# Loading wv by chunks of the model dimension, and V of the first tiles chunk by chunk, in a fused attention and SwiGLU kernel

## The chip, the cores and the metric

The kernel runs on one core of a Trainium2 chip. A core has five instruction streams that run side by side: TensorE (PE in the profile, with its weight loads as PEld), VectorE (DVE), ScalarE (ACT), GpSimd (POOL) and SyncE (SP), which here only issues DMAs. The metric is the device time of one execution in microseconds, as the median of the runs shown. The profile is of one execution.

## What is computed

The input x (2048 tokens, model dimension D = 640, bfloat16) is normalized once, and the result feeds a linear attention of 32 heads of 20 and a SwiGLU layer of 1536, which are added to x.

```python
xn = layernorm(x)                                   # over the 640 columns
q, k, v = split(xn @ wqkv)                          # wqkv: 640 x 1920; v is its last 640 columns
pq, pk  = q @ w_phi, k @ w_phi                      # per head, 20 x 20
phi_q   = concat(softmax(pq), softmax(-pq))         # 40 features to a head
phi_k   = concat(softmax(pk), softmax(-pk))
kv, z   = phi_k.T @ v, sum(phi_k)
A       = ((phi_q @ kv) / (phi_q @ z + 1e-6)) @ wo
B       = (silu(xn @ w1) * (xn @ w3)) @ w2
out     = x + A + B
```

## The kernel before

**Tiles.** The 2048 tokens are 16 tiles of 128. `x_tok` holds a tile with its tokens on the partitions; normalized there, it is transposed to `xnT`, where the model dimension lies on the partitions in DC = 5 chunks of 128. Every projection of a tile is a sum over these five chunks, accumulated in PSUM: `xnT[:, i, tile]` is the stationary operand, rows `i` of the weight are the moving one. PSUM has eight banks of 512 float32 columns, and 640 columns take two of them.

**The order of the work.** No loop order is written out. 14 generators (`norms`, `transposes`, `attention`, `mlps` and so on, from line 729) each offer their next step, a list of instructions; the loop from line 927 works out when each could start, by the planner's own costs (line 353 for a matmul: columns / 2400 + 0.003; 0.06 for a transpose, line 357) and 0.07 for an engine to learn that another is done, and takes the earliest, the stream with the lower rank in a tie. A step with PE work counts as startable at the latest of its operands and PE's free time plus 0.15 (line 945). The steps of `norms` are taken well ahead (`URGENT`, line 921). A step is never split. The instructions of each engine are then played in that order, with semaphore waits where they depend on another engine or a DMA; an engine also waits for its own earlier instruction if it reads what that one writes (line 146).

**The start.** `first_loads` (line 412) issues on SP, in this order: half of x tile 0, tiles 1 and 2, the first part of wv, tile 3, the second part of wv, the first third of w1 and w3, w_phi, the transposing load of wk, and x tiles 4 to 11; the other half of tile 0 goes out on ACT. `warm_up` gives PE filling matmuls on zeros while it waits. `norms` (line 729) works out mean and variance of tiles 0, 2 and 3 on DVE with two `bn_stats` of half a tile each (`ln_half`, line 449) and a `bn_aggr` (in `ln_rstd`, line 453), of tile 1 on ACT; the power -0.5 is POOL's. `ln_apply` (line 492) normalizes the tile in place on DVE. `xn_transpose` (line 511) transposes tiles 0 to 3 on PE and copies the result from PSUM on the engine that the planner expects to be done first; later tiles are transposed by DMA. After tile 0's transposes PE gets eight more filling matmuls.

**V of tiles 0 to 3.** In `attention` (line 814) tiles 0 to 3 are handled apart from the rest: for each tile, once it is transposed, two banks are held, and ten steps `v_part` (line 552) of one matmul each follow, first the five chunks of columns 0 to 383, then the five of columns 384 to 639. This goes with the load: wv comes by columns, all five chunks of columns 0 to 383 first. The 640 results lie one behind the other, from column 128 of the first bank on, so that 384 of them end with it. `v_store` (line 556) copies them to `v2` on ACT. Later tiles use `v_tile` (line 560): ten matmuls of 320 columns, one half of the columns to a bank, and a store over both banks.

After V of tile 3 come two columns of the MLP, the folding of w_phi into wk, and the K projections.

Of the kernel before, what the change touches and what calls it, by code (L numbers as in the profile page):

```python
# [3 lines left out]
ACT = mybir.ActivationFunctionType  # L4
# [5 lines left out]
D = 640  # L10
H = 32
DH = 20
F = 1536
T = S // 128
DC = D // 128
# [232 lines left out]
def bass_parallel_sum__linear_kernel_hedgehog__glu_gated_swiglu__prompt_kernel(  # L248
# [16 lines left out]
    P = _Program(nc)  # L265
# [12 lines left out]
    def new(name, shape, dtype, offset=None):  # L278
        size = mybir.dt.size(dtype)
        for n in shape[1:]:  # L280
            size *= n
        return P.sbuf(name, shape, dtype, region(size) if offset is None else offset)
# [13 lines left out]
    xnT = new("xnT", [128, DC, S], bf)  # L296
# [14 lines left out]
    wv = new("wv", [128, DC, D], bf, RKV + 6400)  # L311
# [14 lines left out]
    v2 = new("v2", [128, T, H * 21], bf, RV)  # L326
# [15 lines left out]
    def bank(k, cols=512, off=0, rows=128):  # L342
        return PS[0:rows, k * 512 + off:k * 512 + off + cols]

    def bank2(k, cols):
        return PS[:, k * 512:(k + 2) * 512].rearrange("p (b c) -> p b c", c=512)[:, :, 0:cols]


    def mm(o, l, r, start, stop, shared=False, cost=None):
        n = free(r)  # L350
        P.op("PE", "matmul", [o], [l, r], (o, l, r),
             dict(start=start, stop=stop, skip_group_check=shared),
             cost=max(n / 2400 + 0.003, 0.055) if cost is None else cost)
# [5 lines left out]
    def free(ap):  # L359
        n = 1  # L360
        for s in ap.shape[1:]:
            n *= s
        return n

    def act(o, i, f, scale=1.0):
        P.op("ACT", "activation", [o], [i], (o, i, f), dict(scale=scale),
             cost=0.17 + free(o) / 1200)
# [32 lines left out]
    wqkv_t = A_wqkv.rearrange("(c p) n -> p c n", p=128)  # L400
# [4 lines left out]
    def w13(a, b):  # L405
        P.dma("SP", w1_s[:, :, a:b], w1_t[:, :, a:b])
        P.dma("SP", w3_s[:, :, a:b], w3_t[:, :, a:b])

    def load_x(a, b):
        P.dma("SP", x_tok[:, a:b, :], x_t[:, a:b, :])  # L410

    def first_loads():
        def part_wv(a, b):
            P.dma("SP", wv[:, :, a:b], wqkv_t[:, :, 2 * D + a:2 * D + b])

        P.dma("SP", x_tok[:, 0, 0:320], x_t[:, 0, 0:320])
        P.dma("ACT", x_tok[:, 0, 320:D], x_t[:, 0, 320:D])
        load_x(1, 2)
        load_x(2, 3)
        part_wv(0, 384)  # L420
        load_x(3, 4)
        part_wv(384, D)
        w13(0, 512)
        P.dma("SP", phi_s[:], phi_t)
        P.dma("SP", wqkT[:, DC:2 * DC, :], A_wqkv[:, D:2 * D], True)
        load_x(4, 8)
        load_x(8, 12)


    def consts():  # L430
        memset("DVE", t1[:, 2, :], 0.0)
        memset("DVE", warm[:], 0.0)
        act(warm[:], warm[:], ACT.Exp)
        memset("POOL", ident[:], 0.0)
        select(ident[:], 0, [[-1, 128]], 1, ALU.not_equal, 1.0)
        memset("POOL", GM[:], 1.0)
        select(GM[:], 0, [[128, DC], [-DH, H]], 1, ALU.is_ge, 0.0)
        select(GM[:], DH, [[-128, DC], [DH, H]], -1, ALU.is_gt, 0.0)
        memset("POOL", mhalf[:], -0.5)
# [9 lines left out]
    def ln_half(t, q):  # L449
        i, o = x_tok[:, t, 320 * q:320 * q + 320], bst[:, t, 6 * q:6 * q + 6]  # L450
        P.op("DVE", "bn_stats", [o], [i], (o, i), cost=0.5)

    def ln_rstd(t0, n):
        for t in range(t0, t0 + n):
            o, i = mv[:, t, 0:2], bst[:, t, 0:12]
            P.op("DVE", "bn_aggr", [o], [i], (o, i), cost=0.22)
        m, v, r, z = mv[:, t0:t0 + n, 0], mv[:, t0:t0 + n, 1], rstd[:, t0:t0 + n, 0], rstd[:, t0:t0 + n, 1]
        if t0 < 4:
            P.op("DVE", "tensor_scalar", [r], [v], (),
                 dict(out=r, in0=v, scalar1=EPS, scalar2=None, op0=ALU.add), cost=0.08)  # L460
        else:
            P.op("POOL", "tensor_scalar_add", [r], [v], (r, v, EPS), cost=0.25)
        P.op("POOL", "tensor_tensor", [r], [r, mhalf[:, 0:n]], (r, r, mhalf[:, 0:n], ALU.pow),
             cost=0.6 if t0 < 4 else 0.73)
        if t0 >= 4:
            P.op("POOL", "tensor_scalar_mul", [z], [m], (z, m, -1.0), cost=0.25)
            P.op("POOL", "tensor_tensor", [z], [z, r], (z, z, r, ALU.mult), cost=0.25)
# [9 lines left out]
    def scalar_op(t, o, i, a, b):  # L477
        P.op("DVE", "tensor_scalar", [o], [i], (),
             dict(out=o, in0=i, scalar1=a, scalar2=b, op0=ALU.mult, op1=ALU.add), cost=0.15)
# [66 lines left out]
    def proj(t, w, k):  # L546
        for q in range(2):
            for i in range(DC):
                mm(bank(k + q, 320), xnT[:, i, t * 128:(t + 1) * 128],
                   w[:, i, 320 * q:320 * q + 320], i == 0, i == DC - 1)  # L550

    def v_part(t, q, i, k):
        a, b = ((0, 384), (384, D))[q]
        mm(bank(k, b - a, 128 + a), xnT[:, i, t * 128:(t + 1) * 128], wv[:, i, a:b], i == 0, i == DC - 1)

    def v_store(t, k):
        act(v2[:, t, :].rearrange("p (h c) -> p h c", c=21)[:, :, 0:DH],
            bank(k, D, 128).rearrange("p (h c) -> p h c", c=DH), ACT.Copy)

    def v_tile(t, k):  # L560
        proj(t, wv, k)
        pv = bank2(k, 320).rearrange("p b (h c) -> p b h c", c=DH)
        act(v2[:, t, :].rearrange("p (b h c) -> p b h c", b=2, c=21)[:, :, :, 0:DH], pv, ACT.Copy)

    def k_tile(t, k):
        proj(t, Wkp, k)
# [161 lines left out]

    def norms():
        yield lambda: (first_loads(), consts())  # L730
        yield lambda: act_sum(1, ACT.Copy, bst[:, 1, 0:1])
        yield lambda: (ln_half(0, 0), ln_half(0, 1), ln_rstd(0, 1))
        yield lambda: scalar_op(1, mv[:, 1, 0:1], bst[:, 1, 0:1], -1.0 / D, 0.0)
        yield lambda: act_sum(1, ACT.Square, mv[:, 1, 1:2], mv[:, 1, 0:1])
        yield lambda: ln_apply(0)
        done["ln"] = 1
        yield lambda: act_rstd(1)
        yield lambda: ln_half(2, 0)
        while done["t"] < 1:
            yield None  # L740
        yield lambda: ln_half(2, 1)
        yield lambda: ln_apply(1)
        done["ln"] = 2
        yield lambda: ln_rstd(2, 1)
        yield lambda: ln_half(3, 0)
        yield lambda: ln_apply(2)
        done["ln"] = 3
        yield lambda: (ln_half(3, 1), ln_rstd(3, 1))
        yield lambda: ln_apply(3)
        done["ln"] = 4  # L750
        yield block_diag
        todo = []
        for t in range(4, T + 2, 2):
            if t == T or t > done["k"] + 8 or t == 12 and done["w"] < 8:
                for u in todo:
                    yield lambda u=u: ln_apply(u)
                    done["ln"] = u + 1
                todo = []
            if t == T:
                break  # L760
            while t > done["k"] + 8 or t == 12 and done["w"] < 8:
                yield None
            yield lambda t=t: ln_stats(t, 2)
            for u in todo:
                yield lambda u=u: ln_apply(u)
                done["ln"] = u + 1
            todo = [t, t + 1]
            if t == 6:
                yield consts_late
# [44 lines left out]
    def attention():  # L814
        def v(t):
            return lambda: v_tile(t, banks(2))

        yield warm_up
        for t in range(4):
            while done["t"] <= t:  # L820
                yield None
            k = banks(2)
            held.add(k // 2)
            for q in range(2):
                for i in range(DC):
                    yield lambda t=t, q=q, i=i, k=k: v_part(t, q, i, k)
            yield lambda t=t, k=k: v_store(t, k)
            held.clear()
        while done["f"] < 1:
            yield None  # L830
        for t in range(T):
            while done["t"] <= t:
                yield None
            yield lambda t=t: k_tile(t, banks(2))
            done["k"] = t + 1
            if t >= 4:
                yield v(t)
            if 9 <= t < 14:
                while done["f"] < 2:
                    yield None  # L840
                yield lambda dc=t - 9: fold_mm(0, dc, banks(2))
        yield lambda: P.dma("SP", wo_s[:], A_wo.rearrange("(c p) d -> p c d", p=128))
        done["v"] = 1
# [83 lines left out]
    while any(alive):  # L927
# [32 lines left out]
        i, ops, after = best[2:]  # L960
# [65 lines left out]
```

## Time and profile before

| | |
|---|---|
| Median of three runs | 271.44 us (270.61 to 271.59) |
| The profiled execution | 271.62 us |
| Its span, first to last instruction | 269.9 us |
| Moved by DMA | 27.73 MB in 63510 packets |
| Read from and written to HBM | 12.81 MB, 2.62 MB |
| Granted TensorE clock, mean | 1.000 |

How to read it: the busy times of the page are sums over the whole span, and engines work side by side. The table by stages says in which stretch an engine stands still, the chain of waits leads back from the last instruction through whatever released each step, and the timeline has the instructions themselves, with consecutive ones of a kind merged (xN); in brackets stands the idle time in front of the first, and what ended it. All work of the kernel has line 102 in the profile, a helper's, so rows are told apart by the names of the tiles: `PS<-ident,x_tok` is a transpose, `PS<-wv,xnT` is V, `PS<-t` is a filling matmul, `PS<-xnT,w_s` is the MLP, `PS<-Wkp,xnT` is K.

### The profile page before, as it was taken

What the parts mean: (1) busy time and instruction counts of PE and PEld (TensorE: products, weight loads), DVE (VectorE), ACT (ScalarE), POOL (GpSimd) and SP (SyncE); (2) the same over time, 40 slices, a digit from 0 to 9 for tenths busy, and PEclk for the clock granted to TensorE, in tenths of its full rate; (3) what the DMA queues carried; (4) which work ended last, traced back from release to release, by engine and by line L of the source; (5) the groups of instructions that cost most, each with busy time, mean ns of one, the idle gap of its engine ahead of it and who ended that gap; (6) DMA issues with size and microseconds to landing.
All of it is one profiled execution on the core that took longest, in us unless ns stands there. A gap on an engine that the chain in (4) does not pass through costs nothing.

```text
span 269.9 us, 4848 instructions
## 1 busy us (share of the span) xinstructions
PE 264.3 (98%) x1978; PEld 161.7 (60%) x1978; DVE 178.2 (66%) x307; ACT 100.6 (37%) x194; POOL 97.7 (36%) x126
## 2 busy tenths in 40 slices
PE   7899999999999999999999999999999999999996
PEld 4556676577765545554554554544677777777774
DVE  4549898999999898788777797777833321212112
ACT  5447988788821634333434423343100000000000
POOL 4125848789994344444213443124420000000000
DMA  6990599970058254531344422444076333131211
GB/s 179 277 278 1 104 307 270 160 188 3 0 168 230 53 101 81 74 58 36 69 78 80 78 39 42 78 79 101 3 99 158 86 85 97 51 97 49 87 37 49
DMA packets 63510, 27.73 MB, mean 103 GB/s; under 512 B 49792, under 2 KB 63488, under 8 KB 63488
## 3 DMA queue, kind: packets, MB, share of 16 engines
q1 hardware_dynamic: 63344, 27.35, 44.2%
q8 instruction: 15, 0.25, 0.4%
q10 hardware_dynamic: 144, 0.08, 0.1%
q14 instruction: 7, 0.06, 0.1%
HBM read 12.81 MB, written 2.62 MB: 57 GB/s over the span
## 4 chain that ended last, share of the span: by engine, by line
PE 87%; DMA 5%; DVE 3%; POOL 2%; SPq 1%; issue 1%
PE PS L102 87%; DMA xnT<-x_tok 3%; DMA wv<-in_A_wqkv_dram 2%; DVE bst L102 1%; POOL rstd L102 1%; POOL v L102 1%; DVE x_tok L102 1%; SPq L114 1%; DVE hT L102 0%; DVE t L102 0%; DVE mv L102 0%; POOL M L102 0%; DVE xres L102 0%; POOL ekt L102 0%
## 5 line engine op out<-in xcount | busy, mean ns | idle before, releaser
L102 PE MATMUL PS<-xnT,w_s 128*128 128x512 bf16 x480 | 108.5, 379 | 0.0
L102 PEld LDWEIGHTS PS<-xnT,w_s 128*128 128x128 bf16 x480 | 45.3, 98 | 50.1 <-DVE t L102 0.4
L102 PE MATMUL PS<-w_s,hT 128*128 128x320 bf16 (+2 forms) x384 | 54.9, 299 | 0.0
L102 POOL TENSOR_TENSOR eq<-eq,rq 128x600 bf16<-128x600 bf16 (+1 forms) x32 | 22.7, 731 | 76.5 <-DVE rq L102 76.3
L102 DVE TENSOR_TENSOR xres<-PS,xres 128x640 bf16<-128x640 f32 (+2 forms) x17 | 13.4, 786 | 55.7 <-PE PS L102 55.7
L102 ACT ACTIVATE th<-PS 128x512 f32<-128x512 f32 x48 | 28.8, 599 | 49.6 <-PE PS L102 49.6
L102 PEld LDWEIGHTS PS<-w_s,hT 128*128 128x128 bf16 x384 | 37.6, 98 | 14.6
L102 DVE SCALAR_TENSOR_TENSOR t<-th,PS 128x512 bf16<-128x512 f32 x48 | 32.6, 679 | 20.1 <-ACT th L102 20.1
L102 POOL TENSOR_TENSOR ekt<-ekt,rS 128x640 bf16<-128x640 bf16 x32 | 39.8, 1280 | 3.1 <-DVE rS L102 3.1
L102 ACT ACTIVATE eq<-PS 128x600 bf16<-128x600 f32 (+1 forms) x72 | 24.6, 412 | 26.2 <-PE PS L102 26.1
L102 DVE SCALAR_TENSOR_TENSOR hT<-t,PS 128x512 bf16<-128x512 bf16 x48 | 33.0, 687 | 1.7
L102 PE MATMUL PS<-wv,xnT 128*128 128x320 bf16 (+2 forms) x160 | 24.6, 299 | 1.1 <-DMA wv<-in_A_wqkv_dram 1.1
L102 ACT ACTIVATE ekt<-PS 128x640 bf16<-128x640 f32 x32 | 22.3, 703 | 6.7 <-PE PS L102 6.2
L102 PE MATMUL PS<-wo_s,oT 128*128 128x320 bf16 (+2 forms) x160 | 24.5, 299 | 0.0
L102 PE MATMUL PS<-Wkp,xnT 128*128 128x320 bf16 x160 | 23.9, 299 | 0.5 <-DMA xnT<-x_tok 0.5
L102 PE MATMUL PS<-Wqp,xnT 128*128 128x512 bf16 (+1 forms) x160 | 24.0, 299 | 0.0
L102 DVE TENSOR_REDUCE S<-ekt 128x64 f32<-128x1280 bf16 x16 | 23.0, 1438 | 0.0
L102 PEld LDWEIGHTS PS<-Wqp,xnT 128*128 128x128 bf16 x160 | 13.2, 98 | 11.9
L102 PEld LDWEIGHTS PS<-wv,xnT 128*128 128x128 bf16 x160 | 15.3, 98 | 7.2 <-ACT xnT L102 1.0
L102 POOL TENSOR_TENSOR half<-eq 128x660 f32<-128x660 bf16 x14 | 19.0, 1359 | 1.2 <-ACT eq L102 1.2
L102 PEld LDWEIGHTS PS<-Wkp,xnT 128*128 128x128 bf16 x160 | 15.4, 98 | 6.8 <-ACT ekt L102 0.8
L102 PEld LDWEIGHTS PS<-wo_s,oT 128*128 128x128 bf16 x160 | 15.5, 98 | 6.1
(55 smaller groups left out, 178.3 us busy)
## 6 DMA issues: line engine op xcount, KB each, us to landing
w_s<-in_B_w_dram SPq DMA_DIRECT2D x6, 640.0 KB, 7.0
xres<-in_A_x_dram SPq DMA_DIRECT2D x16, 160.0 KB, 2.4
out_dram<-xres SPq DMA_DIRECT2D x15, 160.0 KB, 1.8
x_tok<-in_A_x_dram SPq DMA_DIRECT2D x3, 640.0 KB, 6.2
w_s<-in_B_w_dram SPq DMA_DIRECT2D x1, 1920.0 KB, 7.8
wo_s<-in_A_wo_dram SPq DMA_DIRECT2D x1, 800.0 KB, 4.8
x_tok<-in_A_x_dram SPq DMA_DIRECT2D x3, 160.0 KB, 3.6
wv<-in_A_wqkv_dram SPq DMA_DIRECT2D x1, 480.0 KB, 5.5
```

The costliest lines, as they stand in the source:

```text
L102: o = _Op(eng, lambda: m(*args, **kw), r, w, cost)
L114: o = _Op(eng, lambda: m(out, in_), self.regions(in_), self.regions(out), nbytes, True)
```

## The change

wv is loaded by chunks of the model dimension: chunks 0 and 1 with all 640 columns first, chunks 2 to 4 second, at the same two places among the loads. V of tiles 0 to 3 goes chunk by chunk: a step is now two matmuls of 320 columns, one into each of two banks, for one chunk, and there are five steps to a tile. The store of these tiles takes the form of the later ones. In `norms`, tile 1 is applied ahead of the second half of tile 2's statistics instead of behind it.

```diff
     def first_loads():
         def part_wv(a, b):
-            P.dma("SP", wv[:, :, a:b], wqkv_t[:, :, 2 * D + a:2 * D + b])
+            P.dma("SP", wv[:, a:b, :], wqkv_t[:, a:b, 2 * D:3 * D])
...
-        part_wv(0, 384)
+        part_wv(0, 2)
         load_x(3, 4)
-        part_wv(384, D)
+        part_wv(2, DC)
...
-    def v_part(t, q, i, k):
-        a, b = ((0, 384), (384, D))[q]
-        mm(bank(k, b - a, 128 + a), xnT[:, i, t * 128:(t + 1) * 128], wv[:, i, a:b], i == 0, i == DC - 1)
+    def v_part(t, i, k):
+        for q in range(2):
+            mm(bank(k + q, 320), xnT[:, i, t * 128:(t + 1) * 128], wv[:, i, 320 * q:320 * q + 320],
+               i == 0, i == DC - 1)
 
     def v_store(t, k):
-        act(v2[:, t, :].rearrange("p (h c) -> p h c", c=21)[:, :, 0:DH],
-            bank(k, D, 128).rearrange("p (h c) -> p h c", c=DH), ACT.Copy)
+        pv = bank2(k, 320).rearrange("p b (h c) -> p b h c", c=DH)
+        act(v2[:, t, :].rearrange("p (b h c) -> p b h c", b=2, c=21)[:, :, :, 0:DH], pv, ACT.Copy)
 
     def v_tile(t, k):
         proj(t, wv, k)
-        pv = bank2(k, 320).rearrange("p b (h c) -> p b h c", c=DH)
-        act(v2[:, t, :].rearrange("p (b h c) -> p b h c", b=2, c=21)[:, :, :, 0:DH], pv, ACT.Copy)
+        v_store(t, k)
...
         while done["t"] < 1:
             yield None
-        yield lambda: ln_half(2, 1)
         yield lambda: ln_apply(1)
         done["ln"] = 2
+        yield lambda: ln_half(2, 1)
         yield lambda: ln_rstd(2, 1)
...
-            for q in range(2):
-                for i in range(DC):
-                    yield lambda t=t, q=q, i=i, k=k: v_part(t, q, i, k)
+            for i in range(DC):
+                yield lambda t=t, i=i, k=k: v_part(t, i, k)
             yield lambda t=t, k=k: v_store(t, k)
```

## The prediction

> **What bounds the kernel now.** I read the page's first part, then a table of the span by stages, then the chain that ended last, then the first 15 us instruction by instruction.
>
> ```profile
> span 269.9 us, 4848 instructions
> PE 264.3 (98%) x1978; PEld 161.7 (60%) x1978; DVE 178.2 (66%) x307; ACT 100.6 (37%) x194; POOL 97.7 (36%) x126
> ```
>
> TensorE (PE) is busy for 264.3 of 269.9 us, an average. The table by stages shows where the other 5.6 us are (first columns: stretch, its length, PE busy; then PEld, DVE, ACT, POOL, the granted clock, DMA share, GB/s).
>
> ```profile
> 0.00:5.83 5.83, 4.34 (x18) 2.16 (x19) 2.20 (x10) 3.24 (x6) 2.19 (x11) 1.00 0.59 150
> 5.83:9.31 3.48, 2.42 (x23) 1.73 (x24) 2.81 (x10) 0.81 (x2) 1.11 (x2) 1.00 1.09 342
> 9.31:14.55 5.24, 5.24 (x45) 3.90 (x46) 1.46 (x5) 3.11 (x5) 1.65 (x4) 1.00 1.31 251
> 14.55:41.20 26.65, 26.64 (x191) 17.14 (x189) 22.07 (x41) 21.30 (x33) 14.20 (x29) 1.00 0.65 164
> 41.20:42.05 0.85, 0.33 (x4) 0.03 (x2) 0.65 (x2) 0.82 (x2) 0.85 (x2) 1.00 1.27 311
> 42.05:267.40 225.35, 225.34 (x1702) 136.77 (x1702) 148.60 (x242) 71.34 (x149) 77.74 (x82) 1.00 0.39 87
> ```
>
> After the first transpose at 5.83 PE stands still for 3.48 - 2.42 = 1.06 us up to 9.31 and for 0.85 - 0.33 = 0.52 us at 41.2, and nowhere else until 267.4. So a change at the start is worth what it moves the end of the V stage (14.55), provided that what follows moves with it. The chain of waits says that it does:
>
> ```profile
> 3.23 6.04 DMA wv<-in_A_wqkv_dram
> ...
> 9.31 10.05 PE PS L102 x71
> 19.36 0.67 DVE hT L102
> ...
> 33.72 8.19 DMA xnT<-x_tok
> ...
> 42.05 225.35 PE PS L102 x1702
> ```
>
> The second part of wv, issued at 3.23, lands at 9.27 and releases PE; PE's end of the second MLP column releases VectorE (19.36), which leads to the transposing DMA that ends the wait at 42. That wait hangs on PE's early work, so it slides with it.
>
> Now the stage itself, from the timeline:
>
> ```profile
> 6.34 0.66 PE L102 MATMUL PS<-t 128*128 128x128 bf16 x8
> ...
> 7.87 0.81 PE L102 MATMUL PS<-wv,xnT 128*128 128x384 bf16 x4 [0.87 <-DMA wv<-in_A_wqkv_dram]
> ...
> 8.51 0.44 PE L102 MATMUL PS<-ident,x_tok 128*128 128x128 bf16 x5
> ...
> 9.31 1.04 PE L102 MATMUL PS<-wv,xnT 128*128 128x256 bf16 x7 [0.20 <-DMA wv<-in_A_wqkv_dram]
> ...
> 10.19 0.44 PE L102 MATMUL PS<-ident,x_tok 128*128 128x128 bf16 x5
> ...
> 10.47 1.85 PE L102 MATMUL PS<-wv,xnT 128*128 128x384 bf16 x12
> ...
> 12.16 0.44 PE L102 MATMUL PS<-ident,x_tok 128*128 128x128 bf16 x5
> ...
> 12.64 0.49 DVE L102 COPY xnT<-PS 128x640 bf16<-128x640 bf16 x1 [1.63 <-PE PS L102]
> ...
> 13.18 1.25 PEld L102 LDWEIGHTS PS<-wv,xnT 128*128 128x128 bf16 x10 [0.16 <-DVE xnT L102]
> ...
> 14.55 4.48 PE L102 MATMUL PS<-xnT,w_s 128*128 128x512 bf16 x20
> ```
>
> Two landings of wv release PE, at 7.87 and 9.31; the transposes of tiles 1, 2, 3 (T1, T2, T3) stand at 8.51, 10.19, 12.16. T3's copy back gates V of tile 3 (13.18), and the first MLP matmul follows at 14.55.
>
> **The loads.** Part one shrinks from 480 to 320 KB (chunks 0 and 1, all columns), part two grows from 320 to 480 KB; the sum, the order of the issues and their number stay, and the rows in DRAM become 1280 bytes instead of 768 and 512. The DMA rate by stage (last column):
>
> ```profile
> 3.25:4.00 0.75, 0.75 (x3) 0.30 (x2) 0.71 (x2) 0.40 (x1) 0.00 (x0) 1.00 0.86 140
> 4.00:4.75 0.75, 0.75 (x7) 0.55 (x6) 0.63 (x4) 0.45 (x3) 0.03 (x1) 1.00 0.78 110
> 4.75:6.25 1.50, 1.25 (x13) 0.99 (x12) 0.91 (x3) 0.90 (x2) 0.88 (x2) 1.00 0.96 323
> 6.25:7.50 1.25, 0.74 (x11) 0.57 (x9) 0.92 (x3) 0.49 (x1) 0.23 (x1) 1.00 1.11 338
> 17.00:19.00 2.00, 2.00 (x13) 0.94 (x12) 1.22 (x3) 0.60 (x1) 0.00 (x0) 1.00 1.03 371
> ```
>
> wv moves at 323 to 338 GB/s (take 331), the later load of x in 1280-byte rows at 371. The 960 KB (983 kB) of part one, x tile 3 and part two take 983/331 = 2.97 us, and would take 983/371 = 2.65: 0.32 us less. Ahead of wv is a hole: 3.25 to 4.75 runs at 125 GB/s on average, 0.19 MB where 331 GB/s would have carried 0.50, so 1.5 x (1 - 125/331) = 0.93 us are lost as the first load with several rows to a partition gets under way. The trace doesn't show what two or three rows to a partition do. Bounds: the hole vanishes (0.93 earlier), or part two, which now touches three fifths of wv's rows for the first time, brings a second one (0.93 later). I leave the hole as it is, between ends equally far, because both parts still have several rows to a partition. Part one, 320 KB at 371 instead of 480 KB at 331 GB/s (0.88 us instead of 1.48), releases PE 0.60 earlier than 7.87, at 7.27. So part two releases PE at S = 9.31 - 0.32 = 8.99; bounds 8.06 and 9.92.
>
> The Trainium skill ("DMA: Bandwidth & Descriptors", Specifications) puts the least transfer for line rate at 512 bytes; by that the longer rows gain nothing, S stays 9.31 and the sum below is +0.88. The rows disagree, 338 against 371 GB/s, and I go by them.
>
> **PE work behind S.** Today only five 256-column matmuls of tile 0 wait for part two; then six of 320 do (chunks 2 to 4, two halves). Cost of one: eight of the same shape in the K stage below, (1.25 - 0.30)/7 = 0.136 us apart.
>
> ```profile
> 42.05 1.25 PE L102 MATMUL PS<-Wkp,xnT 128*128 128x320 bf16 x8 [0.52 <-DMA xnT<-x_tok]
> ```
>
> **The two banks.** They cost nothing: 384 + 256 columns at offset 128 already lay in two banks, the columns per tile stay 640, and the store in the new form, which later tiles use already, takes what the old one takes:
>
> ```profile
> 10.07 0.71 ACT L102 ACTIVATE v<-PS 128x640 bf16<-128x640 f32 x1 [0.37 <-PE PS L102]
> ...
> 10.67 0.70 ACT L102 ACTIVATE xnT<-PS 128x640 bf16<-128x640 bf16 x1
> ...
> 36.13 0.71 ACT L102 ACTIVATE v<-PS 128x640 bf16<-128x640 f32 x1
> ```
>
> **Tile 1 ahead of tile 2's second statistics.**
>
> ```profile
> 3.18 1.02 DVE L102 BATCH_NORM_STATS2 bst<-x_tok 128x6 f32<-128x320 bf16 x2 [1.98 <-DMA x_tok<-in_A_x_dram]
> 4.24 0.21 DVE L102 BATCH_NORM_AGGREGATE mv<-bst 128x2 f32<-128x12 f32 x1
> ...
> 6.79 0.48 DVE L102 BATCH_NORM_STATS2 bst<-x_tok 128x6 f32<-128x320 bf16 x1
> ...
> 7.19 0.43 DVE L102 TENSOR_SCALAR x_tok<-x_tok,mv,rstd 128x640 bf16<-128x640 bf16 x1
> ...
> 7.54 0.20 DVE L102 BATCH_NORM_AGGREGATE mv<-bst 128x2 f32<-128x12 f32 x1
> ...
> 10.56 0.45 DVE L102 TENSOR_SCALAR x_tok<-x_tok,mv,rstd 128x640 bf16<-128x640 bf16 x1 [0.67 <-POOL rstd L102]
> ```
>
> The apply moves from 7.19 to about 6.8, so T1 can run near 7.5, behind V0's first chunk, in time in which PE would wait for part two. No instruction is added and no DMA moves. The other way round, the aggregate now follows its statistics directly and must wait for their end (4.20 to 4.24 above) instead of overlapping the apply: about 7.72 instead of 7.54, so tiles 2 and 3 are applied 0.2 us later. Tile 3 would then be ready near 11.2, and PE asks for it (below) at S + 3.71 = 12.7: hidden. Without that cover it would cost 0.2.
>
> **Where the planner puts the transposes.** Only the order comes from its costs, no time. A step of V was one matmul (0.163 or 0.110 in its units); it is now two of 320 (0.273, both inseparable). By hand from the unchanged point, PE free at 7.16 and tile 0's copy done on DVE at 6.86: T1 can go at 7.38, so chunk 0 of V0 first, then T1. V0 ends at 8.83. The aggregate's wait puts T2's readiness at 9.51: two chunks of V1, then T2, three chunks. V2 begins at 10.66, T3 is ready at 11.64; after three chunks PE is free at 11.47 and the fourth chunk would start at 11.62 by the planner's rule, ahead of T3: four chunks (eight matmuls), then T3, then the fifth. Today T3 stands behind four matmuls of V2, 0.65 us; eight take 1.09. This is the step that speaks against the change.
>
> **The sum, from S.** Chunks 2 to 4 of V0: 6 x 0.136 = 0.82. Two chunks of V1: S + 1.36. T2: 0.28 to the next matmul (10.19 to 10.47), its result after 0.44, so S + 1.80; ScalarE copies it from S + 1.84 to S + 2.54. V1's other three chunks end at S + 1.64 + 0.82 = S + 2.46; V2 starts at S + 2.62 (0.08 from copy to matmul, as around 13.18): a wait of 0.16. Four chunks: S + 3.71. T3: result at S + 4.15, copy of 0.49 from S + 4.19 to S + 4.68; PE, done with the fifth chunk at S + 4.26, waits 0.5 us. V3 from S + 4.76, 10 x 0.136: S + 6.12. Today the same stretch is 14.55 - 9.31 = 5.24. Change: 0.88 + (S - 9.31) = 0.88 - 0.32 = **+0.56 us**.
>
> So V starts earlier, T1 fills a gap, and most of that is given back as the wait for T3's copy. The profiled execution took 271.62 us (span 269.9 and 1.72 around it) and would become 272.18; it stands 0.18 above the median of 271.44, so on the median's scale 272.0.
>
> **Rivals.**
>
> B, the loads come early: S from 8.06 to 8.6, so -0.37 to +0.17 against today, about 271.3. For it: the hole stands ahead of 640 rows, and only 256 come first afterwards. Against: the x load has rows as long and its own slow start isn't told apart here.
>
> C, part two brings its own hole: S from 9.5 to 9.92, +1.07 to +1.49, about 272.7. For it: new rows; against: by then the engines have work queued.
>
> D, the other side: PE's clock falls. It decides if PE works too little ahead of S. Place: PE is done with its filling matmuls at 7.00 (6.34 + 0.66), waits 0.27 us for part one, works 0.82 (four matmuls of V and T1) and waits 0.90 for part two.
>
> ```profile
> 1.24 4.34 PE L102 MATMUL PS<-t 128*128 128x512 bf16 x18 [1.24 <-DVE warm L102]
> ```
>
> Seven matmuls of 512 and eleven of 128 columns (4992) took 4.34 us there, against 20 of 512 (10240) in 4.48 at 14.55: about half the speed at the start, though the rows give a clock of 1.00. A second such stretch of 4.3 us would cost 2.2: 274.2. Against: today's 1.06 us of gaps cost no speed. The Trainium skill ("TensorE: Matmul & The Clock Gate", Part 1) has the clock fall after an idle window of about 3.4 us; by it D would not happen, and the trace agrees as far as gaps of 1 us go.
>
> E, the planner's order behind 14.55 changes. Its PE clock is some 0.07 later there and most costs move alike, so I expect the old order; a new one could close the 0.52 us wait at 41.2 or open another as long: 271.5 or 272.5, more if several change.
>
> **Chances and range.** My forecast 0.50 (S from 8.6 to 9.5, +0.17 to +1.07: 271.6 to 272.5), B 0.17, C 0.13, D 0.08, E 0.12. Half a per cent, 1.36 us, is about what can be told from no change. Slower by more: D 0.08, C's upper end 0.06, E 0.05, mine 0.03, together 0.22. Faster by more needs nearly all of PE's 1.06 + 0.52 us of waits: E 0.05, B 0.04, together 0.09. The rest, 0.69, is no change. Range: from B's end with the wait at 41.2 closed, 271.44 - 0.37 - 0.52 = 270.5, to C's end, 272.93, and 0.3 for the run: 273.2; it leaves out D and part of E.
>
> **What would show it.** T1 near 7.5 and ahead of V0's second chunk; part two's wait ending near 9.0; eight V matmuls between V2's start and T3; a wait of 0.5 us for the copy of tile 3; first MLP matmul near 15.1; the wait near 42 still there, later by as much. Wrong if S lies outside 8.6 to 9.5, if T3 stands earlier, if PE's 512-column matmuls lie more than 0.22 us apart after S, or if what follows 15 doesn't slide.

## The result, and the profile after

| | before | changed |
|---|---|---|
| Median, 23 runs each | 270.94 us (270.26 to 273.05) | 272.09 us (270.89 to 274.43) |
| Ratio changed to before | | 1.0036, 95% interval 1.0023 to 1.0048 |
| Beside each other again (30 and 7 runs, another chip) | 271.03 us | 272.15 us, ratio 1.0031 (1.0019 to 1.0043) |
| And again (33 and 10 runs, a third chip) | 270.94 us | 272.26 us, ratio 1.0046 (1.0027 to 1.0066) |

The changed kernel is slower by 0.98 us (0.0036 x 270.94; 0.62 to 1.30 by the interval). That is within half a per cent, but the interval lies wholly above 1. The quotient of the two medians is 1.0042; the ratio in the table is nearer to that of the means of all runs (1.0035), and the text goes by the ratio.

The first profile of the changed kernel (span 272.7 us, the slowest of the 23 runs) is not a typical one. This is its table by stages, with the columns as in the table by stages of the kernel before; the first number behind the five engines is the granted clock:

```profile
5.65:7.80 2.15, 2.01 (x22) 1.47 (x22) 1.70 (x6) 0.79 (x3) 0.56 (x1) 1.00 0.83 247
7.80:9.53 1.73, 0.24 (x3) 0.01 (x1) 1.43 (x5) 0.70 (x1) 0.55 (x1) 1.00 1.04 356
9.53:12.67 3.14, 3.14 (x15) 2.00 (x16) 0.88 (x4) 0.71 (x1) 0.55 (x1) 0.51 1.44 231
12.67:15.25 2.58, 2.58 (x23) 1.76 (x21) 0.00 (x0) 1.41 (x2) 1.72 (x5) 0.93 1.08 242
15.25:17.38 2.13, 1.77 (x12) 1.09 (x12) 0.49 (x1) 0.72 (x2) 0.25 (x1) 1.00 0.95 230
```

TensorE's clock fell to about half from 9.53, when the second part of wv arrived, to about 13: rival D of the prediction, in this one run. So the chain is read in the second profile (a1 below, span 269.9 us, clock 1.000). TensorE from tile 0's V to the MLP there:

```profile
6.80 0.45 PE L102 MATMUL PS<-wv,xnT 128*128 128x320 bf16 x2
7.35 0.45 PE L102 MATMUL PS<-ident,x_tok 128*128 128x128 bf16 x5
7.64 0.43 PE L102 MATMUL PS<-wv,xnT 128*128 128x320 bf16 x2
8.35 1.53 PE L102 MATMUL PS<-wv,xnT 128*128 128x320 bf16 x10 [0.28 <-DMA wv<-in_A_wqkv_dram]
9.72 0.44 PE L102 MATMUL PS<-ident,x_tok 128*128 128x128 bf16 x5
10.00 2.22 PE L102 MATMUL PS<-wv,xnT 128*128 128x320 bf16 x14
12.05 0.44 PE L102 MATMUL PS<-ident,x_tok 128*128 128x128 bf16 x5
12.34 0.43 PE L102 MATMUL PS<-wv,xnT 128*128 128x320 bf16 x2
13.08 1.53 PE L102 MATMUL PS<-wv,xnT 128*128 128x320 bf16 x10 [0.31 <-DVE xnT L102]
14.45 2.32 PE L102 MATMUL PS<-xnT,w_s 128*128 128x512 bf16 x10
```

S stands for the moment at which the second part of wv releases TensorE, V0 to V3 for the matmuls of V of tiles 0 to 3. The order is the one of the prediction, step for step: one chunk of V0, T1, the second chunk, S (8.35), three chunks and two of V1 (ten matmuls), T2, fourteen matmuls (three chunks of V1, four of V2), T3, the last two of V2, a wait for T3's copy, V3. From S to the first MLP matmul it takes 14.45 - 8.35 = 6.10 us, against 5.24 before. The wait for T3's copy shows as 0.31 us in brackets, counted from the end of the last matmul; by the starts it is 13.08 - 12.34 - 2 x 0.136 = 0.47 us. Behind this stage nothing new is to be seen; the wait near 42 is still there, at 0.67 us here and 0.44 in the third profile of the same kernel:

```profile
42.10 1.11 PE L102 MATMUL PS<-Wkp,xnT 128*128 128x320 bf16 x7 [0.67 <-DMA xnT<-x_tok]
```

### The profile page after: what moved, and what is told of

It reads as the page before. It is cut to its first block, busy times and chain, and to the rows that moved or that the text cites. A ratio compares the mean times of both kernels' runs of the same rounds, so it can differ in the third digit from the quotient of the medians.

```text
span 272.7 us, 4828 instructions
## 1 busy us (share of the span) xinstructions
PE 264.9 (97%) x1958; PEld 162.2 (59%) x1978; DVE 178.5 (65%) x307; ACT 100.7 (37%) x194; POOL 97.6 (36%) x126
## 4 chain that ended last, share of the span: by engine, by line
PE 87%; DMA 5%; DVE 3%; POOL 2%; issue 1%; SPq 1%
PE PS L102 87%; DMA xnT<-x_tok 3%; DMA wv<-in_A_wqkv_dram 2%; DVE bst L102 1%; POOL rstd L102 1%; POOL v L102 1%; DVE x_tok L102 1%; SPq L114 1%; DVE hT L102 0%; DVE t L102 0%; DVE xnT L102 0%; DVE mv L102 0%; POOL M L102 0%; DVE xres L102 0%; POOL ekt L102 0%
## 5 line engine op out<-in xcount | busy, mean ns | idle before, releaser
L102 PE MATMUL PS<-xnT,w_s 128*128 128x512 bf16 x462 | 105.1, 379 | 1.2 <-ACT Wkp L102 0.2
L102 PE MATMUL PS<-wv,xnT 128*128 128x320 bf16 x160 | 26.2, 312 | 1.8 <-DMA wv<-in_A_wqkv_dram 1.5
L102 PE MATMUL PS<-Wqp,xnT 128*128 128x128 bf16 (+1 forms) x158 | 23.6, 298 | 0.1
```

The source lines that it names most:

```text
L102: o = _Op(eng, lambda: m(*args, **kw), r, w, cost)
```

## The experiments

Twelve kernels, four at a time on a chip, each timed in five rounds beside the kernel before. Theories: A, the order of the work behind S (the forecast's sum); B, the clock; C, the loads alone; L, later loads that go out too early. How often the clock fell is counted from all runs of a kernel (those that show a mean below 0.997).

| | what differs | ratio to before, 95% interval | clock fell |
|---|---|---|---|
| a1 | the changed kernel again | 1.0031 (1.0019 to 1.0043) | 0 of 7 |
| a2 | before, tile 1 applied early | 1.0009 (0.9995 to 1.0022) | 0 of 12 |
| a3 | changed, tile 1 not applied early | 1.0039 (1.0022 to 1.0056) | 2 of 12 |
| a4 | changed, wv by columns | 1.0047 (1.0020 to 1.0074) | 3 of 12 |
| b1 | changed, T3 earlier | 0.9999 (0.9983 to 1.0015) | 0 of 12 |
| b2 | changed, wv four chunks and one | 1.0052 (1.0023 to 1.0081) | 4 of 12 |
| b3 | changed, later loads held back | 1.0026 (1.0008 to 1.0043) | 0 of 12 |
| b4 | a4 with filling matmuls | 1.0069 (1.0047 to 1.0092) | 0 of 6 |
| c1 | the changed kernel a third time | 1.0046 (1.0027 to 1.0066) | 0 of 10 |
| c2 | as b1 | 1.0021 (1.0007 to 1.0035) | 0 of 12 |
| c3 | c2, x tile 3 loaded last | 1.0008 (0.9995 to 1.0021) | 0 of 12 |
| c4 | c3, wv three chunks and two | 0.9985 (0.9973 to 0.9997) | 0 of 12 |

**a1, the changed kernel again.**

> The changed kernel once more, because TensorE's granted clock fell to half for 3.4 us in its first profile. S is the moment when the second part of wv releases TensorE (9.31 us before the change, 9.53 in the first profile after it). Theory A (my order of the work): the loss is work behind S and the wait for tile 3's copy, so without the clock's fall the first MLP matmul comes at S + 6.1, near 15.6, the span is 270.3 to 270.9 and the ratio 1.003 to 1.005. Theory B (clock): the loss is the clock; the granted clock is below 1 between 9 and 13 us again, span over 272. Theory C (loads): all of the loss is that S is later; S + 5.24 ends the stage, so S would have to be 10.2 or later.

Measured: S at 8.35 in the profile and the MLP 6.10 later, clock 1.000 in all seven runs, ratio 1.0031, spans 269.9 to 270.8. The 15.6 for the MLP was a miss, it came at 14.45, because S didn't stay near 9.5. B falls as the cause of the loss: without the clock's fall the loss is still there. C, all of the loss a later S, falls too: the stretch behind S takes 6.10 us and not 5.24. S is earlier in this profile than in the one of before (9.31), and the stage ends at the same time (14.45 and 14.55).

**a2, the swap alone.**

```diff
-        yield lambda: ln_half(2, 1)
         yield lambda: ln_apply(1)
         done["ln"] = 2
+        yield lambda: ln_half(2, 1)
```

> The kernel before with tile 1's normalization ahead of tile 2's second statistics and nothing else. Theory A: the planner now puts the transposes of tile 3 behind five matmuls of tile 2's V instead of four; worked through like the forecast, with S still 9.31, the stage ends at S + 5.46 instead of S + 5.24: +0.2 us, ratio 1.0008 (0.9995 to 1.002). Theory B: 0, the clock stays at 1. Theory C: 0.

Measured: 1.0009, which takes in the forecast and also zero. The profile (TensorE) settles the mechanism:

```profile
9.56 1.21 PE L102 MATMUL PS<-wv,xnT 128*128 128x256 bf16 x8 [0.97 <-DMA wv<-in_A_wqkv_dram]
10.60 0.44 PE L102 MATMUL PS<-ident,x_tok 128*128 128x128 bf16 x5
10.88 1.95 PE L102 MATMUL PS<-wv,xnT 128*128 128x384 bf16 x12
12.66 0.44 PE L102 MATMUL PS<-ident,x_tok 128*128 128x128 bf16 x5
12.94 2.28 PE L102 MATMUL PS<-wv,xnT 128*128 128x256 bf16 x15
15.06 1.68 PE L102 MATMUL PS<-xnT,w_s 128*128 128x512 bf16 x7
```

Between T2 and T3 stand twelve matmuls, and V2's first five are among them, one more than before. 15.06 - 9.56 = 5.50 us, 5.46 expected. So by itself the swap shows no gain.

**a3, the change without the swap** (a2's edit the other way round in the changed kernel).

> The changed kernel with the old place of tile 1's normalization. Theory A: tile 1's transposes go behind the third chunk of tile 0 and so behind S, tile 1's V then waits for its copy, but tile 3's transposes stand behind two chunks of tile 2's V instead of four; by the same arithmetic the stage ends at S + 6.15, no more than 0.1 us from the changed kernel: ratio to before 1.003 to 1.005. If the swap is what costs, this is nearer to 1.000; if it is what helps, above 1.006. Theory B: less work ahead of S (0.55 us instead of 0.82), so the clock falls more often. Theory C: as the changed kernel.

Measured: 1.0039. The profile has T1 behind S, as expected, and the MLP 15.34 - 9.17 = 6.17 us after S (6.15 expected):

```profile
9.17 0.45 PE L102 MATMUL PS<-wv,xnT 128*128 128x320 bf16 x2 [1.73 <-DMA wv<-in_A_wqkv_dram]
9.45 0.44 PE L102 MATMUL PS<-ident,x_tok 128*128 128x128 bf16 x5
...
15.34 1.46 PE L102 MATMUL PS<-xnT,w_s 128*128 128x512 bf16 x6
```

So whether T1 fills the gap or not made no measurable difference here: by the order in the two profiles, what it saves is given back because T3 then goes later. The clock fell in two runs, which took 273.4 and 273.5 us against 272.0 for the median of the other ten.

**a4, the change with the old loads.**

```diff
-            P.dma("SP", wv[:, a:b, :], wqkv_t[:, a:b, 2 * D:3 * D])
+            P.dma("SP", wv[:, :, a:b], wqkv_t[:, :, 2 * D + a:2 * D + b])
...
-        part_wv(0, 2)
+        part_wv(0, 384)
...
-        part_wv(2, DC)
+        part_wv(384, D)
```

> The changed kernel with wv loaded by columns as before (384, then 256), so that the whole of V of the first tile stands behind the second part. Theory A: S back at 9.3, 1.36 us of tile 0 behind it instead of 0.82, tile 3's transposes behind three chunks of tile 2's V; the stage ends at S + 6.39, 15.7: +1.15 us, ratio 1.0042 (1.003 to 1.0055). Theory C: S back at 9.31 takes the loss away: 1.000. Theory B: only tile 1's transposes ahead of S, so the clock falls in many runs and the ratio is over 1.006.

Measured: 1.0047; the ratio holds three runs in which the clock fell (274.2 to 274.7 us), the other nine have a median of 271.71. C falls once more: the old loads don't bring the old time. In the profile S was 8.47, from 8.47 to the MLP at 14.70 it took 6.23 us, 0.16 less than worked out. With the clock at 1 the loss of 0.68 us is below the 1.15 forecast for it, and below the 6.23 - 5.24 = 0.99 by which the stretch behind S is longer; S would have to lie some 0.3 us earlier in these runs than in the kernel before, which no run shows by itself.

**b1 and c2, T3 earlier.** The planner subtracts 0.5 from the time of T3's step and takes it behind two chunks of V2.

```diff
                 at = max(P.ready(ops, i in (QUERIES, QTOKS)), P.free["PE"] + 0.15)
+                if i == 1 and done["t"] == 3:
+                    at -= 0.5
```

> The changed kernel with the transposes of tile 3 taken 0.5 us earlier by the planner, so behind two chunks of tile 2's V instead of four; nothing else moves on any engine but the copy behind it. Theory A (order of the work): tile 3's copy is done when tile 2's V ends, the wait of 0.5 us goes and the stage ends at S + 5.6 instead of S + 6.1: ratio to before 1.0015 (1.0003 to 1.0028). Theory C (only the loads matter): as the changed kernel, 1.003 to 1.004.

> The kernel of b1 (tile 3's transposes behind two chunks of tile 2's V) beside the changed kernel, to size its gain. Theory A: 0.5 us faster than c1, 0.4 us slower than before where S is the same (stage S + 5.6 against S + 5.24): ratio 1.0005 to 1.002. If the gain of 0.9 us between a1 and b1 holds, the loads of the new form must come earlier than the old ones by about as much as was forecast (0.3 us), and the ratio is 0.9985 to 1.0005.

Measured: b1 0.9999, below the 1.0003 to 1.0028 expected of it; c2 1.0021, just above the 1.0005 to 1.002 of theory A and well above the 0.9985 to 1.0005 that would have gone with earlier loads. Beside c1's 1.0046 on the same chip that is 0.0025 x 270.94 = 0.68 us faster than the changed kernel, where 0.5 was expected; the two intervals overlap (1.0027 to 1.0066, 1.0007 to 1.0035), so the size is loose. Between chips (a1 and b1) it seemed to be 0.9. In b1's profile S came at 8.00, the earliest of all. In c2's profile (TensorE) sixteen matmuls follow T3 and none of them waits for a copy:

```profile
8.56 1.53 PE L102 MATMUL PS<-wv,xnT 128*128 128x320 bf16 x10 [0.59 <-DMA wv<-in_A_wqkv_dram]
9.93 0.44 PE L102 MATMUL PS<-ident,x_tok 128*128 128x128 bf16 x5
10.21 1.68 PE L102 MATMUL PS<-wv,xnT 128*128 128x320 bf16 x10
11.72 0.44 PE L102 MATMUL PS<-ident,x_tok 128*128 128x128 bf16 x5
12.00 2.34 PE L102 MATMUL PS<-wv,xnT 128*128 128x320 bf16 x16
```

V3 ends at 12.00 + 16 x 0.136 = 14.18, S + 5.62, as worked out (5.6), where the changed kernel has S + 6.10. The wait for T3's copy was real and, by the profiles, worth about half a microsecond.

**b2, four chunks and one.** `part_wv(0, 4)` and `part_wv(4, DC)`.

> The changed kernel with wv split after the fourth chunk (640 KB, then 160 KB) instead of after the second; the order on TensorE is the same. Theory A: one chunk of tile 0 stands behind S instead of three, the stage ends at S + 5.57; with S unchanged the ratio is 1.0015 (1.0003 to 1.0028), lower still if the small second part comes sooner. If the second part's own slow start is what holds it (theory C), the first part now carries four fifths of the rows and S should come earlier too: ratio below 1.001.

Measured: a miss, 1.0052, with the clock down in four of twelve runs (273.8 to 274.3 us; the others' median is 271.88). The first part, 640 KB, now lands last in effect: TensorE has no work at all until it comes.

```profile
6.42 0.61 PE L102 MATMUL PS<-t 128*128 128x128 bf16 x8
8.27 0.43 PE L102 MATMUL PS<-wv,xnT 128*128 128x320 bf16 x2 [1.23 <-DMA wv<-in_A_wqkv_dram]
8.54 0.44 PE L102 MATMUL PS<-ident,x_tok 128*128 128x128 bf16 x5
8.82 1.79 PE L102 MATMUL PS<-wv,xnT 128*128 128x320 bf16 x12
```

The wait moved from the second part to the first; the expectation had forgotten it.

**b3, the later loads held back.** The loads of w_phi and wk go out in a step of their own behind `ln_apply(1)`, the first of them waiting for its result.

> The changed kernel with the loads of w_phi and wk held back on SP until tile 1 is normalized on VectorE (about 7.2 us), near the time at which they went out before the change (6.34 and 7.72); in the changed kernel they go out at 4.8 and 5.3, because its loads have half as many rows. The order on every engine is the same. Theory L (loads that go out early take the second part's place): S falls from 8.9 to 8.5 as in the kernel before and the ratio to 1.0018. Theory C (the second part starts slowly by itself): S and the ratio stay, 1.003 to 1.004.

Measured: 1.0026 (1.0008 to 1.0043), between what L and C expected; the two loads went out at 7.09 and 7.51, and S was 8.71 in the profile. It decides nothing between the two.

**b4, a4 with filling matmuls.** Twenty matmuls of zeros stand ahead of tile 0's V; they write a bank that V doesn't use yet.

> The kernel of a4 (wv by columns, V chunk by chunk), in which the granted clock fell in 3 of 12 runs, with 20 filling matmuls of 128 columns ahead of tile 0's V while TensorE waits for wv; they feed nothing. Theory B (the clock falls where too little work stands in the window ahead of S): no run of 12 shows a clock below 0.998, and the median stays as it was, ratio 1.002 to 1.0035, with a narrower interval. If the clock falls for another reason, two or three runs show 0.994 again and take some 2.5 us longer.

Measured: the clock didn't fall in six runs, but 0 of 6 is thin beside 3 of 12, and the kernel got slower, not the same: 1.0069. The fillers ran for 2.15 us from 6.37 and pushed T1 to 8.37, and S was 9.24 in the profile. The first MLP matmul came at 15.70, 1.00 us later than in a4's profile, 0.77 of it from S. Beside the kernel before on their own chips, b4 loses 273.02 - 271.16 = 1.86 us and a4's runs at full clock 0.68, so some 0.2 us stay open, and so does why S came later.

**c1, c3 and c4.** c3 issues x tile 3 behind the second part of wv; c4 also uses `part_wv(0, 3)` and `part_wv(3, DC)`.

> The changed kernel beside the next three on one chip. Ratio to before 1.0025 to 1.0045; the first MLP matmul at S + 6.1 again, whatever S is.

> c2 with x tile 3 loaded behind the second part of wv instead of ahead of it; the order on the four engines is the same. 160 KB less lie ahead of S, 0.45 us at the rate of the page: S earlier by that much, 0.3 to 0.5 us faster than c2. Against it: tile 3's first statistics stand ahead of tile 2's normalization on VectorE and now wait for x tile 3 until about 9; if that holds up tile 2's transposes, the gain is gone.

> c3 with three chunks of wv in the first part and two in the second, so that 0.27 us less of tile 0's V stands behind S, and 0.27 more ahead of it. Theory A: another 0.25 us faster than c3 as long as the first part lands before about 7.6; the granted clock doesn't fall. This is the version that should be faster than the kernel before: ratio 0.997 to 0.9995.

Measured: c1 1.0046, just above the 1.0045 expected, with S 8.94 and the MLP at 15.04 (S + 6.10); c3 1.0008, 0.35 us (0.0013) faster than c2, and tile 2's transposes weren't held up (1.37 us behind S in both profiles); c4 0.9985, as expected, 0.62 us (0.0023) faster than c3 where 0.25 was expected, and faster than the kernel before, 270.66 against 270.94 us, by its interval though only just. In c4's profile nothing waits for the second part of wv:

```profile
7.16 0.43 PE L102 MATMUL PS<-wv,xnT 128*128 128x320 bf16 x2 [0.26 <-DMA wv<-in_A_wqkv_dram]
7.43 0.44 PE L102 MATMUL PS<-ident,x_tok 128*128 128x128 bf16 x5
7.71 1.79 PE L102 MATMUL PS<-wv,xnT 128*128 128x320 bf16 x12
9.34 0.44 PE L102 MATMUL PS<-ident,x_tok 128*128 128x128 bf16 x5
9.62 1.68 PE L102 MATMUL PS<-wv,xnT 128*128 128x320 bf16 x10
11.19 0.45 PE L102 MATMUL PS<-ident,x_tok 128*128 128x128 bf16 x5
```

From 7.16 on TensorE works without a gap up to V2, where c3's profile still waits 0.27 us for the second part. From the first matmul of V to the first of the MLP c3's profile takes 14.10 - 7.01 = 7.09 us and c4's 13.65 - 7.16 = 6.49, and the 0.60 us between them is almost all time in which c3's TensorE stood still: counted by the starts, 0.44 us ahead of the second part and 0.10 ahead of T1. That c4 really gained more than expected isn't shown: the medians are 0.48 us apart, and c3's runs alone spread over 1.7 us.

## Why the prediction was right or wrong, point by point

**The order.** Right: worked by hand from the planner's costs, it came out on TensorE as predicted, with T3 behind eight matmuls of V2.

**The work behind S and the wait for T3's copy, +0.88.** Right. 6.10 us from S to the MLP in two profiles (8.35 to 14.45, 8.94 to 15.04), 6.12 predicted, 5.24 before: +0.86. The arithmetic also gave 5.46, 6.15 and 5.6 for three variants, and their profiles had 5.50, 6.17 and 5.62 (a2, a3, c2). Other profiles end with 0.2 us more, because the first MLP matmul comes that much behind the last of V, for a reason that the profiles don't show, among them the first one of the changed kernel (17.38 - 15.80 against 1.36), b3 with the changed kernel's order (15.03 - 8.71 = 6.32) and b1 (13.83 - 8.00 = 5.83).

**The swap.** Right in its costs. VectorE in the second profile:

```profile
6.84 0.45 DVE L102 TENSOR_SCALAR x_tok<-x_tok,mv,rstd 128x640 bf16<-128x640 bf16 x1
7.21 0.49 DVE L102 BATCH_NORM_STATS2 bst<-x_tok 128x6 f32<-128x320 bf16 x1
7.72 0.21 DVE L102 BATCH_NORM_AGGREGATE mv<-bst 128x2 f32<-128x12 f32 x1
...
10.73 0.45 DVE L102 TENSOR_SCALAR x_tok<-x_tok,mv,rstd 128x640 bf16<-128x640 bf16 x1 [0.66 <-POOL rstd L102]
...
12.54 0.49 DVE L102 COPY xnT<-PS 128x640 bf16<-128x640 bf16 x1 [1.36 <-PE PS L102]
```

The aggregate starts at 7.72, as worked out; tile 3 is ready at 11.2 and asked for at 12.05: hidden.

**The loads, S = 9.31 - 0.32.** This is the term that was mis-sized. The forecast subtracted it from 0.88 and got +0.56; +0.98 was measured (0.62 to 1.30 by the interval), so the loads brought the changed kernel no such gain. S in single profiles can't tell: of the changed kernel alone they have 9.53, 8.35 and 8.94, so one execution differs from the next by more than the 0.32 in question. Two of the three lie outside the 8.6 to 9.5 that the prediction itself had named as its sign of being wrong, one on either side; and the 9.31 from which the forecast started was itself late.

The spans of all runs tell more. From the first MLP matmul to the end it is 255.35 us before (269.9 - 14.55), 255.45 in a1 and 255.26 in c1, so the median spans beside each other on a1's chip, 269.3 and 270.4 us, put that matmul at 13.95 and 15.05, and S at 13.95 - 5.24 = 8.71 before and 15.05 - 6.10 = 8.95 changed (taking it that the second part releases TensorE in both). On c1's chip (269.2 and 270.5) it is 8.61 and 9.05. By this S was 0.2 to 0.4 us later, where 0.32 earlier was forecast. The lateness isn't firm: the stretch from the MLP to the end varies from 254.87 us (b1) to 255.70 (c3) over the profiles, and b1 speaks the other way, since its stretch behind S is 5.62 - 5.24 = 0.38 us longer than before by c2's rows and its time is the same (0.9999).

The DMA rates (last column) of a1 by stage:

```profile
3.25:4.75 1.50, 1.50 (x9) 0.85 (x8) 1.17 (x4) 0.74 (x2) 0.14 (x1) 1.00 0.88 245
4.75:6.25 1.50, 1.36 (x14) 1.10 (x13) 0.84 (x4) 1.01 (x3) 0.43 (x2) 1.00 0.92 313
6.25:7.50 1.25, 1.15 (x15) 0.73 (x14) 1.17 (x4) 0.49 (x1) 0.56 (x1) 1.00 0.85 266
```

Of both things that the prediction bounded equally far, a part came true. The hole of 3.25 to 4.75 is smaller (245 GB/s in a1, 259 in c1; before, 125 in the one profile that the prediction had, 193 to 221 in a2, a4 and b4, which load wv as before). The first part, a third smaller, came forward, to 6.1 us in a1 (issued at 2.20, 3.9 us to landing) from 7.7, earlier than the 7.27 forecast, so the 0.27 us that TensorE was to wait for it didn't come up. And under the second part the rate fell (at 6.25 to 7.50 it was 212 to 266 GB/s in five of the six profiles with the new loads and 332 in b1, against 284 to 338 in the four with the old ones). Over the whole stretch the two cancel. These are the kernel before and a4, with the old loads, then c1 and b1, with the new ones:

```profile
3.25:7.50 4.25, 3.50 (x27) 2.41 (x25) 3.17 (x11) 2.24 (x5) 1.14 (x2) 1.00 0.95 258
3.25:7.50 4.25, 2.67 (x29) 1.75 (x28) 3.20 (x11) 2.24 (x5) 1.13 (x2) 1.00 0.94 279
```

```profile
3.25:7.50 4.25, 4.00 (x32) 2.76 (x31) 3.35 (x11) 2.24 (x5) 1.13 (x2) 1.00 0.82 254
3.25:7.50 4.25, 4.01 (x34) 2.74 (x33) 3.24 (x11) 2.24 (x5) 1.14 (x2) 1.00 0.94 291
```

All four profiles with the old loads (before, a2, a4, b4) have 258 to 284 GB/s there, six with the new ones (the changed kernel's three, a3, b1, c2) 254 to 291; the rates are of all loads in flight. So the step of the forecast that failed is the one from 331 to 371 GB/s: with rows of 1280 bytes the start moved no faster than with rows of 768 and 512. The second part landed between 8.42 and 9.51 us in the four profiles (9.10 on average) and between 7.95 and 9.48 in the six (8.71). That looks like the forecast gain, but the four were executions mostly slower than their kernels' others. If each landing is set back by how far its execution lay from the median of its kernel's runs at full clock, as if that distance were all S, the averages are 8.65 and 8.75 (without the first profile of the changed kernel, whose clock fell): no gain. What lowers the rate under the second part (the first touch of its rows, or the loads behind it that now go out earlier) is open; b3 didn't separate them. The Trainium skill's 512 bytes for line rate ("DMA: Bandwidth & Descriptors", Specifications) would have left S where it was and given the +0.88, which lies nearer to the measured +0.98; these rates agree with it as far as they go.

**The number.** That 272.0 us was forecast and 272.09 measured is luck. The forecast started from 271.44, the median of three runs, and the median of 23 is 270.94; this 0.50 made up for a change that was forecast too small.

**The banks and the store at nothing.** Nothing in the profiles speaks against it: the store still takes 0.71 us. It was not tried alone.

**What follows slides.** Right for the changed kernel: 255.35 us from the MLP to the end before, 255.45 and 255.26 after, and the wait for the transposing DMA, at 42 in the kernel before, is there in its three profiles (0.74, 0.67 and 0.44 us). So rival E isn't seen.

**The rivals.** D, the clock, came in 1 of the changed kernel's 40 runs, and that run was at 274.43 us (274.2 forecast for it). Of B and C each had a part of the loads right, a smaller hole ahead of the first part and a slower second part, but neither time came: about 271.3 for B, 272.7 for C, whose +1.07 to +1.49 lies above the measured +0.98.

## What to carry to other kernels

Split a load so that the work which can start on the first part fills the time until the second comes, and count what is left behind the second part: here each chunk left behind it costs 0.27 us (two matmuls of 0.136). When the steps of a planner get coarser, look at what they now keep waiting: two matmuls to a step put a transpose 0.44 us later, and its copy became a wait of half a microsecond. A landing time or a rate from one profile is a sample; look at several profiles and at the spans of all runs before an estimate of a few tenths rests on it.

## What the runs showed of the hardware that was not expected

TensorE's clock can fall to about half for some 3 us (0.51 from 9.53 to 12.67) although TensorE had not been idle for long; the prediction had given that a chance of 0.08. In the first profile after the change it had 2.25 us of work in the 3.88 us from 5.65 to 9.53 (2.01 + 0.24 in the table of stages), and stood still for no longer than 1.49 us at a stretch:

```profile
7.61 0.43 PE L102 MATMUL PS<-wv,xnT 128*128 128x320 bf16 x2
9.53 2.82 PE L102 MATMUL PS<-wv,xnT 128*128 128x320 bf16 x10 [1.49 <-DMA wv<-in_A_wqkv_dram]
```

The ten matmuls took 2.82 us there, 1.53 in a1. How often it fell went with how little TensorE had to do ahead of S: 4 of 12 runs with nothing between the fillers and 8.27 (b2), 3 of 12 with T1 and one matmul (a4), 2 of 12 with four matmuls (a3), 1 of 40 with four and T1 (the changed kernel), 0 of 36 in b1, b3 and c2, which have the same work there. The kernel before, timed beside them, had it once in 92 runs (273.32 us, mean clock 0.994). The first three counts can't be told from each other, but together, 9 of 36, they stand out. A run in which it fell took 1.5 to 3.0 us more than the median of its kernel's other runs. The Trainium skill ("TensorE: Matmul & The Clock Gate", Part 1) has the clock fall after an idle window of about 3.4 us; the slow stretch is about as long as that window, but no window here was idle throughout. How much work keeps the clock up is open, and the sum of it isn't all: b2's profile had 2.23 us of work in the 3.87 us up to 8.27, and a3's stood still for 1.73 us at a stretch, and in both the clock stayed at 1.00 afterwards. It was not tried by itself.
